# Masked attention and an MLP: the high and low parts of the last 64 keys in one moving tile

## The chip, the core and the metric

One core of a Trainium2 chip runs the whole program. The metric is the device time in microseconds of one execution. The core's engines are TensorE (PE, with its weight loads as PEld), VectorE (DVE), ScalarE (ACT), GpSimd (POOL) and SyncE (SP, which issues the DMAs). Each works through its own instructions in order; they wait for each other through semaphores.

## The reference

Attention over 8 batches, 8 heads, 576 positions and head size 64, in which each row keeps only the scores within `tau` of the row's maximum, followed by a two-layer MLP on 4608 tokens (512 to 2048 to 512):

```python
def _attn_ref(q, k, v, tau) -> np.ndarray:
    scale = 1.0 / np.sqrt(q.shape[-1])
    scores = scale * np.matmul(q, k.transpose(0, 1, 3, 2))
    thresh = np.max(scores, axis=-1, keepdims=True) - tau
    scores = np.where(scores >= thresh, scores, -1000000000.0)
    scores = scores - np.max(scores, axis=-1, keepdims=True)
    attn = np.exp(scores)
    attn = attn / (np.sum(attn, axis=-1, keepdims=True) + 1e-09)
    return np.matmul(attn, v).astype(np.float32)

def _moe_ref(x, w_in, w_out, alpha) -> np.ndarray:
    h = x @ w_in
    g = np.maximum(h, 0.0) + alpha * np.minimum(h, 0.0)
    return (g @ w_out).astype(np.float32)
```

## The kernel before

**Pairs and units.** The 64 heads are taken in 32 pairs. A pair has nine units: four blocks of 128 queries for each of the two heads (`j` = 0, 1), and a unit "t" (number 4) that holds the last 64 queries of both. Unit 1, 3, 6 and 8 are those of head 1 in the four query blocks. For a unit, PE computes the scores into PSUM (`scores`), DVE takes the row maximum (`rowmax`, tile `nmx`), ACT the exponential (`expo`, tile `p`, and the threshold `thr`), and DVE masks and sums (`mask`). Two PSUM buffers hold scores, so the scores of unit i+2 need the mask of unit i.

**Turning p.** The product with v needs p with the keys on the partitions. PE transposes the unit's p in four chunks of 128 keys (`turn`, PSUM tile `t`). 576 keys are four such chunks and 64 more: 512 keys of head 0 from the front with its last 64 left over, and 512 keys of head 1 from the back with its first 64 left over. The two left-over pieces lie side by side in `p`, and one transpose (`turn_k`, PSUM tile `tk`, and `tk_t` for unit 4) brings both: head 0's 64 keys on partitions 0 to 63, head 1's on 64 to 127. It is done once per query block, at the units of head 1 and at "t".

**Two parts.** Products run in fp32r, a narrower format than fp32. From pair 4 on (`WHOLE` = 4), p and v are split into a high and a low part. ACT copies the transposed p out of PSUM with rounding (`hi` for the four chunks, `hi_k` for the left-over keys; both at L513), and DVE subtracts that from PSUM to give the low part (`lo`, `lo_k`, both at L517). Pairs 0 to 3 run in whole fp32 and have one part.

The tiles: `E0`, `EO` and `O1` hold the four chunks, `TT[step]` the left-over keys of both heads for two query blocks (`step` 0 or 1), one tile for each part. `v` is laid out by the host in ten slots of 128 rows: eight are the chunks; slot 8 has head 0's last 64 keys in rows 0 to 63 and zeros below, slot 9 zeros and then head 1's first 64. So a product with slot 8 and the whole `TT` tile adds only head 0's keys. Its weights have 128 columns, the high and the low part of v side by side, so one pass gives both.

**The product.** `avmul(step, j)` is one accumulation group on PE: for each part, four chunks and one `TT` tile, ten products for a pair in two parts. There are four groups per pair, two with 256 columns, (0, 0) and (1, 1), and two with 322, (0, 1) and (1, 0). ACT brings the two halves of the result out (`avout`: `xa` at L575 and `xb` at L577).

**The order of work** is written out by hand. In cycle i (nine to a pair; the loop at L831), from cycle 52 on:

- PE: `scores(i+2)`, `turn(i)`, `turn_k(i)`, then some layer-2 products of the MLP (`acca`, L237), then what is due in this cycle, such as an `avmul`, and in some cycles a layer-1 group (`pha`, L207).
- DVE: `mask(i)`, `lo_k(i-1)`, `lo(i-1)`, what is due (the MLP's `pta`, the reciprocals `rv`, `rb`), `rowmax(i+2)`.
- ACT: what is due (`avout`, the MLP's `pra`, the roundings `kh`, `vst`, `qst` for the next pairs), `hi_k(i)`, `hi(i)`, `expo(i+2)` and `thr`.

Before cycle 52 two cycles are worked together. The groups of a pair in two parts are due in cycles 5 and 6 of its own pair, (0, 0) and (0, 1), and in cycles 1 and 2 of the next, (1, 1) and (1, 0) (`AVS`). How much MLP work goes into a cycle is decided by constants (`CYCLE`, `busy`, `TH1` to `TH3`) when the program is built. All transposes, products, layer-1 groups and `acca` share four PSUM buffers (`ps_m`).

After the attention the rest of the MLP runs, with the remaining weights split on DVE, ACT and POOL as they arrive; layer 1 and layer 2 of the larger part of the hidden units end the program.

Of the kernel before, what the change touches and what calls it, by code (L numbers as in the profile page):

```python
# [21 lines left out]
P = 128  # L22
D = 64
S = 576
NKC = 4
# [30 lines left out]
WHOLE = 4  # L56
# [7 lines left out]
def f(ap):  # L64
    return ap.bitcast(F32)
# [10 lines left out]
def tile_masked_attention_moe(  # L76
# [11 lines left out]
    nc = tc.nc  # L88
# [17 lines left out]
    part = [dram.tile([n, DM], F32, name=f"part{t}") for t, n in groups1]  # L106

    class Split64:


        def __init__(self, pool, raw, temp_pool, temp, eng, src, a, name, split=False):
            self.split = split
            self.pool, self.raw_tag, self.temp_pool, self.temp_tag = pool, raw, temp_pool, temp
            self.eng = [nc.vector if e == 'v' else nc.gpsimd for e in eng]
            self.src, self.a, self.name = src, a, name
# [75 lines left out]
    def split_x(pool, xr, t0, n, gn, bufs):  # L191
        xh = pool.tile([P, NCC, gn], F32R, tag="xh", name=f"xh{gn}_{t0}", bufs=bufs)
        nc.scalar.activation(xh[:, :, :n], xr[:, :, :n], AF.Copy)  # L193
        xl = pool.tile([P, NCC, gn], F32R, tag="xl", name=f"xl{gn}_{t0}", bufs=bufs)
        nc.gpsimd.tensor_tensor(xl[:, :, :n], xr[:, :, :n], f(xh[:, :, :n]), op=ALU.subtract)  # L195
        return xh, xl
# [60 lines left out]
    class Turned:  # L257


        def __init__(self, pool, dtype, parts):  # L260
            self.parts = range(parts)
            self.EO = [pool.tile([P, 2, NKC, 322], dtype, name=f"eo{parts}{i}") for i in self.parts]
            self.E0 = [pool.tile([P, NKC, 256], dtype, name=f"e0{parts}{i}") for i in self.parts]
            self.O1 = [pool.tile([P, NKC, 256], dtype, name=f"o1{parts}{i}") for i in self.parts]
            self.TT = [[pool.tile([P, 322], dtype, name=f"tt{s}{parts}{i}") for i in self.parts] for s in range(2)]
            for i in self.parts:
                nc.gpsimd.memset(f(self.TT[0][i][:, 2 : 2 + D]), 0.0)
                nc.gpsimd.memset(f(self.TT[1][i][:, 256:320]), 0.0)
                one = 1.0 - i
                nc.gpsimd.memset(f(self.TT[0][i][:, :2]), one)  # L270
                nc.gpsimd.memset(f(self.TT[1][i][:, 320:]), one)
                nc.gpsimd.memset(f(self.EO[i][:, 0, :, 320:]), one)
                nc.gpsimd.memset(f(self.EO[i][:, 1, :, :2]), one)

# [5 lines left out]
    class Pair:  # L280
# [216 lines left out]
        def places_k(self, u):  # L497
            qc, j = UNITS[u]
            if u not in self.K:
                return []  # L500
            kb = self.K[u]
            if qc == "t":
                return [
                    (kb[:D, D:], [self.set.TT[0][i][D:, 2 : D + 2] for i in self.set.parts]),
                    (kb[:D, :D], [self.set.TT[1][i][:D, 256:320] for i in self.set.parts]),
                ]
            step, qi = divmod(qc, 2)
            c0 = qi * P + (D + 2 if step == 0 else 0)
            return [(kb, [self.set.TT[step][i][:, c0 : c0 + P] for i in self.set.parts])]

        def put_hi(self, places):
            for ps, dst in places:
# [32 lines left out]
        def avmul(self, step, j, cs=range(5)):  # L545
            z = self.set
            if (step, j) == (0, 0):
                rhs, tr, col, n = z.E0, [t[:, D + 2 :] for t in z.TT[0]], 2, 256
            elif (step, j) == (0, 1):
                rhs, tr, col, n = [t[:, 1] for t in z.EO], z.TT[0], 0, 322  # L550
            elif (step, j) == (1, 0):
                rhs, tr, col, n = [t[:, 0] for t in z.EO], z.TT[1], 258, 322
            else:
                rhs, tr, col, n = z.O1, [t[:, :256] for t in z.TT[1]], 322, 256
            if cs[0] == 0:
                pa = ps_m.tile([P, 512], F32, tag="pm", name=f"av{self.pi}_{j}_{col}")
                self.av[step, j] = pa, col, n
            pa = self.av[step, j][0]
            m = self.vst.shape[2]
            for part in z.parts:  # L560
                for c in cs:
                    w = self.vst[:, j * NKC + c if c < NKC else 8 + j, :]
                    x = rhs[part][:, c, :] if c < NKC else tr[part]
                    nc.tensor.matmul(  # L564
                        pa[:m, :n], w, x, start=(part == 0 and c == 0), stop=(part == z.parts[-1] and c == NKC)
                    )

        def avout(self, step, j):
            if (step, j) == (0, 0):
# [66 lines left out]
    for p in pairs:  # L636
        o = 9 * p.pi
        n = o - 9
# [167 lines left out]
    for n_, (w, fc, io) in enumerate(pieces):  # L806
        c = n_ * DEC_LAST // (len(pieces) - 1)
# [107 lines left out]
    for t0 in range(0, NT, G2):  # L915
        n = min(G2, NT - t0)
        pool = (wp2, mp2)[t0 // G2 % 2]
        xr = load_x(pool, t0, n, G2, 1)
        x = split_x(pool, xr, t0, n, G2, 1)
        g = [hidden(mp2, ps_2, G2, fc, n, x, f"b{t0}_{fc}", nf) for fc in fcs2]  # L920
        for o in range(0, n, P):
            m = min(P, n - o)
# [14 lines left out]
def lay_out(inputs):  # L937
    import numpy as np

    q, k, v = (np.asarray(inputs[n]) for n in ("q", "k", "v"))  # L940
    b, h, s, d = q.shape
    a = {}
    for n, t in (("q", q), ("k", k)):
        a[n] = np.ascontiguousarray(t.reshape(b, h // 2, 2, s, d).transpose(0, 1, 2, 4, 3)).reshape(b, h // 2, P, s)
    a["k"] = np.concatenate([a["k"], a["k"][..., :d]], axis=-1)
    vv = np.zeros((b, h // 2, P, 10, d), v.dtype)
    v5 = v.reshape(b, h // 2, 2, s, d)
    n = NKC * P
    vv[:, :, :, :4] = v5[:, :, 0, :n].reshape(b, h // 2, NKC, P, d).transpose(0, 1, 3, 2, 4)
    vv[:, :, :, 4:8] = v5[:, :, 1, d:].reshape(b, h // 2, NKC, P, d).transpose(0, 1, 3, 2, 4)  # L950
    vv[:, :, :d, 8] = v5[:, :, 0, n:]
    vv[:, :, d:, 9] = v5[:, :, 1, :d]
    a["v"] = vv
    a["tau"] = np.asarray(inputs["tau"]).reshape(1)
    for n in ("moe_w_in", "moe_w_out"):
        w = np.ascontiguousarray(inputs[n])
        assert w.dtype == np.float64
        a[n] = w.view(np.int64)
    al = np.asarray(inputs["moe_alpha"])
    a["moe_alpha"] = np.ascontiguousarray(al.reshape(-1, P).T)  # L960
    return a
# [22 lines left out]
```

## Time and profile before

| | |
|---|---|
| device time, 3 runs | 1398.99, 1400.43, 1400.41 us; median 1400.41 |
| span of the profiled execution | 1399.2 us |
| PE busy | 1342.0 us, 96% |
| DVE busy | 975.0 us, 70% |
| ACT busy | 820.8 us, 59% |
| POOL busy | 774.5 us, 55% |

The span is the time from the first to the last instruction of one profiled execution; its own total time is not listed beside the three timed runs, which lie between 0.2 us below and 1.2 us above the span. Busy shares are means over the whole span; the stages differ, so the prediction reads them by stage. In a line of a group or of the timeline, "out<-in" names the tiles, the shapes are partitions x elements, and a note in brackets is the idle time of that engine just before, with what ended it. Matmuls are pipelined: a matmul's own duration is longer than the distance to the next one.

### The profile page before, as it was taken

To read this page: it belongs to the slowest core of one execution; us is meant where nothing else is said; L and a number is where in the kernel's file an instruction comes from. 1 tells how busy PE (TensorE), PEld (TensorE's weight loads), DVE (VectorE), ACT (ScalarE), POOL (GpSimd) and SP (SyncE) were. 2 spreads that over 40 slices of the span, in tenths; PEclk is the share of its full clock that TensorE was granted. 3 is DMA by queue.
4 is the path that set the end of the run, shared out by engine and by line. 5 is a ranking of instruction groups with operands and counts; after the bars stand their busy time and mean duration, and the time that the engine had idled before them with its cause. 6 is when DMAs were issued, how large, how long until landed. Compare 5 with 4: busy or idle time off the path is not lost.

```text
span 1399.2 us, 23363 instructions
## 1 busy us (share of the span) xinstructions
PE 1342.0 (96%) x8116; PEld 1184.1 (85%) x8116; DVE 975.0 (70%) x1933; ACT 820.8 (59%) x1843; POOL 774.5 (55%) x879
## 2 busy tenths in 40 slices
PE   5888899999999999999999999898999999999998
PEld 4555889999999999999999998776888888888887
DVE  6999888889888888898888857986333323323332
ACT  7887888888888888888888854453112012111100
POOL 3887576576666666676676557666434224223311
PEclk9999899999999999999999999999999999999999
DMA  7653644644545444454454315333320220111011
GB/s 239 177 148 102 164 113 117 175 116 132 149 120 149 138 135 137 131 146 126 128 157 135 90 56 152 123 118 128 121 69 22 90 90 31 60 61 40 21 61 38
DMA packets 94630, 157.69 MB, mean 113 GB/s; under 512 B 14160, under 2 KB 39024, under 8 KB 94512
## 3 DMA queue, kind: packets, MB, share of 16 engines
q1 hardware_dynamic: 94512, 156.19, 38.3%
q8 instruction: 65, 1.06, 0.3%
q14 instruction: 53, 0.43, 0.1%
HBM read 85.53 MB, written 28.46 MB: 81 GB/s over the span
## 4 chain that ended last, share of the span: by engine, by line
PE 78%; DVE 8%; ACT 4%; DMA 4%; POOL 3%; issue 2%; SPq 1%; POOLq 0%; DVEq 0%; ACTq 0%
PE phb L207 16%; PE accb L237 16%; PE av L564 10%; PE s L417 10%; PE pha L207 9%; PE acca L237 9%; PE t L461 7%; DMA wri<-in_moe_w_in_dram 2%; DVE p L452 1%; DVE nmx L432 1%; PE tk L477 1%; ACT xb L577 1%; DVE wto L142 1%; ACT xa L575 1%; ACT xh L193 1%
## 5 line engine op out<-in xcount | busy, mean ns | idle before, releaser
L432 DVE TENSOR_REDUCE nmx<-s 128x1 f32<-128x576 f32 x288 | 217.1, 754 | 74.9 <-PE s L417 72.0
L228 ACT ACTIVATE gb<-ptb 128x512 fp32r<-128x512 f32 x81 | 50.9, 630 | 337.3 <-DVE ptb L900 336.9
L231 POOL TENSOR_TENSOR gb<-ptb,gb 128x512 fp32r<-128x512 f32 x81 | 104.5, 1291 | 256.5 <-ACT gb L228 256.3
L237 PE MATMUL acca<-wo,ga 128*128 128x512 f32 x756 | 229.5, 418 | 6.8 <-ACT ga L228 3.5
L237 PE MATMUL accb<-wo,gb 128*128 128x512 f32 x972 | 221.9, 389 | 0.0
L237 PEld LDWEIGHTS accb<-wo,gb 128*128 128x128 f32 x972 | 182.6, 188 | 37.8
L452 DVE SCALAR_TENSOR_TENSOR p<-s,thr,p 128x576 f32<-128x576 f32 x256 | 206.8, 808 | 4.0 <-ACT thr L445 3.8
L207 PE MATMUL pha<-xh,wi 128*128 128x256 f32 x1008 | 201.2, 285 | 4.8 <-DVE pta L900 4.5
L207 PE MATMUL phb<-xh,wi 128*128 128x512 f32 x648 | 202.5, 391 | 0.4 <-ACT xh L193 0.4
L440 ACT ACTIVATE p<-s,nmx 128x576 f32<-128x576 f32 x256 | 190.0, 742 | 11.5 <-DVE nmx L432 11.5
L417 PE MATMUL s<-kh,qst 128*128 128x288 f32 x640 | 142.7, 313 | 37.4 <-DVE p L452 22.0
L207 PEld LDWEIGHTS pha<-xh,wi 128*128 128x128 f32 x1008 | 164.8, 192 | 11.1 <-DVE pta L900 6.1
L237 PEld LDWEIGHTS acca<-wo,ga 128*128 128x128 f32 x756 | 132.3, 191 | 27.9 <-POOL ga L231 5.0
L461 PE MATMUL t<-ident,p 128*128 128x128 f32 x1024 | 155.6, 275 | 0.0
L417 PEld LDWEIGHTS s<-kh,qst 128*128 128x128 f32 x640 | 101.8, 193 | 61.1 <-issue 31.7
L930 DVE TENSOR_TENSOR ob<-accb,pin 128x512 f32<-128x512 f32 x36 | 24.2, 689 | 181.5 <-PE accb L237 181.5
L207 PEld LDWEIGHTS phb<-xh,wi 128*128 128x128 f32 x648 | 122.4, 189 | 26.6 <-ACT xh L193 0.8
L207 PE MATMUL pha<-xl,wi 128*128 128x256 f32 x504 | 142.8, 283 | 0.0
L899 DVE TENSOR_SCALAR ptb<-phb,alpha_sb 128x512 f32<-128x512 f32 x81 | 60.7, 751 | 108.1 <-PE phb L207 96.4
L417 PE MATMUL s<-kl,qst 128*128 128x288 f32 x640 | 134.3, 300 | 0.0
L207 PE MATMUL phb<-xl,wi 128*128 128x512 f32 x324 | 127.1, 392 | 3.6 <-POOL xl L195 3.6
L461 PEld LDWEIGHTS t<-ident,p 128*128 128x128 f32 x1024 | 127.2, 142 | 0.1
(124 smaller groups left out, 2789.7 us busy)
## 6 DMA issues: line engine op xcount, KB each, us to landing
kr<-in_k_dram SPq DMA_DIRECT2D x31, 320.0 KB
rb<-rvd SPq DMA_DIRECT2D x64, 144.0 KB
xs<-xa SPq DMA_DIRECT2D x32, 288.0 KB
part<-po SPq DMA_DIRECT2D x36, 256.0 KB
pin<-part SPq DMA_DIRECT2D x36, 256.0 KB
out_dram<-ob SPq DMA_DIRECT2D x36, 256.0 KB
vr<-in_v_dram SPq DMA_DIRECT2D x28, 320.0 KB
qr<-in_q_dram SPq DMA_DIRECT2D x31, 288.0 KB
```

The lines of the kernel that those rows point to most:

```text
L207: nc.tensor.matmul(ph[:, :n], w[:, c, :], xx[:, c, :n], start=(c == 0 and ti == 0), stop=(c == NCC - 1 and ti == 2),)
L228: nc.scalar.activation(g[:, 0, :n], t[:, :n], AF.Copy)
L231: nc.gpsimd.tensor_tensor(g[:, 1, :n], t[:, :n], f(g[:, 0, :n]), op=ALU.subtract)
L237: nc.tensor.matmul(acc[:m, :], gg[:, g, o : o + m], w, start=(first and ti == 0), stop=(last and ti == 2))
L417: nc.tensor.matmul(ps[:, h, :288], w, kk[:, a + h * 288 : a + (h + 1) * 288], start=(ki == 0 and i == 0), stop=(ki == 1 and i == n - 1),)
L432: nc.vector.tensor_reduce(self.nmx[:, j : j + 1], self.S[u][0][:, :, :288], axis=AX.XY, op=ALU.max, negate=True)
L440: nc.scalar.activation(pj, ps[:, :, :288], AF.Exp, bias=nmx[:, j : j + 1], scale=1.0)
L452: nc.vector.scalar_tensor_tensor(pj, ps[:, :, :288], thr[:, j : j + 1], pj, op0=ALU.is_ge, op1=ALU.mult, accum_out=self.sm[:, c : c + 1])
L461: nc.tensor.transpose(tb[:, c, :], pt[:, j, j * D + c * P : j * D + (c + 1) * P], ident)
L564: nc.tensor.matmul(pa[:m, :n], w, x, start=(part == 0 and c == 0), stop=(part == z.parts[-1] and c == NKC))
L899: nc.vector.tensor_scalar(t[:, :n], ph[:, :n], 0.0, alpha_sb[:, fc : fc + 1], op0=ALU.min, op1=ALU.mult)
L930: nc.vector.tensor_tensor(ob[:m], acc[:m], pi_[:m], op=ALU.add)
```

## The change

For pairs in two parts the `TT` tiles give way to tiles `R[step][j]`, one for each group. Such a tile holds, for head j's left-over 64 keys, the high part on that head's 64 partitions and the low part on the other 64. In `v`, slots 8 and 9 of these pairs repeat the same 64 rows in both halves instead of zeros in one. One product with that slot then adds the high and the low part, and a group has nine products instead of ten. To fill the tiles, `places_k` gives two places per block (one for each head, 64 partitions each) where there was one of 128 partitions, and `lo_k` writes to the other half of the partitions from the one it reads. For unit "t" the number of places stays at two. Pairs 0 to 3 compute as before, and the order of the cycles is the same.

```diff
+            if parts == 1:
+                self.TT = [pool.tile([P, 322], dtype, name=f"tt{s}{parts}") for s in range(2)]
...
+            else:
+                self.R = [[pool.tile([P, n], dtype, name=f"rt{s}{j}") for j, n in enumerate(w)] for s, w in enumerate(((256, 322), (322, 256)))]
+                for j, x in ((0, self.R[1][0][:, 320:]), (1, self.R[0][1][:, :2])):
+                    nc.gpsimd.memset(f(x[j * D : (j + 1) * D]), 1.0)
+                    nc.gpsimd.memset(f(x[(1 - j) * D : (2 - j) * D]), 0.0)
...
+            h = [slice(0, D), slice(D, P)]
+            if not self.whole:
+                R = self.set.R
+                if qc == "t":
+                    a, b = R[0][1][:, 2 : D + 2], R[1][0][:, 256:320]
+                    return [(kb[:D, D:], [a[h[1]], a[h[0]]]), (kb[:D, :D], [b[h[0]], b[h[1]]])]
+                step, qi = divmod(qc, 2)
+                out = []
+                for jj in range(2):
+                    c0 = qi * P + (D + 2 if (step, jj) == (0, 1) else 0)
+                    x = R[step][jj][:, c0 : c0 + P]
+                    out.append((kb[h[jj]], [x[h[jj]], x[h[1 - jj]]]))
+                return out
...
-            return [(kb, [self.set.TT[step][i][:, c0 : c0 + P] for i in self.set.parts])]
+            return [(kb, [self.set.TT[step][:, c0 : c0 + P]])]
...
-            for part in z.parts:
-                for c in cs:
-                    w = self.vst[:, j * NKC + c if c < NKC else 8 + j, :]
-                    x = rhs[part][:, c, :] if c < NKC else tr[part]
-                    nc.tensor.matmul(
-                        pa[:m, :n], w, x, start=(part == 0 and c == 0), stop=(part == z.parts[-1] and c == NKC)
-                    )
+            mms = [(part, c) for part in z.parts for c in cs if c < NKC] + [(0, c) for c in cs if c == NKC]
+            for part, c in mms:
+                w = self.vst[:, j * NKC + c if c < NKC else 8 + j, :]
+                x = rhs[part][:, c, :] if c < NKC else tr
+                nc.tensor.matmul(pa[:m, :n], w, x, start=(part == 0 and c == 0), stop=c == NKC)
...
     vv[:, :, :d, 8] = v5[:, :, 0, n:]
     vv[:, :, d:, 9] = v5[:, :, 1, :d]
+    w = vv.reshape(b * (h // 2), P, 10, d)
+    w[WHOLE:, d:, 8] = w[WHOLE:, :d, 8]
+    w[WHOLE:, :d, 9] = w[WHOLE:, d:, 9]
```

More of the change, by code (lines that the diff above doesn't have):

```diff
@@ L264, in __init__ @@
             self.O1 = [pool.tile([P, NKC, 256], dtype, name=f"o1{parts}{i}") for i in self.parts]
-            self.TT = [[pool.tile([P, 322], dtype, name=f"tt{s}{parts}{i}") for i in self.parts] for s in range(2)]
+            if parts == 1:
+                self.TT = [pool.tile([P, 322], dtype, name=f"tt{s}{parts}") for s in range(2)]
+                nc.gpsimd.memset(f(self.TT[0][:, 2 : 2 + D]), 0.0)
+                nc.gpsimd.memset(f(self.TT[1][:, 256:320]), 0.0)
+                nc.gpsimd.memset(f(self.TT[0][:, :2]), 1.0)
+                nc.gpsimd.memset(f(self.TT[1][:, 320:]), 1.0)
+            else:
[3 more added lines that the diff above has]
+                    nc.gpsimd.memset(f(x[(1 - j) * D : (2 - j) * D]), 0.0)
             for i in self.parts:
-                nc.gpsimd.memset(f(self.TT[0][i][:, 2 : 2 + D]), 0.0)
-                nc.gpsimd.memset(f(self.TT[1][i][:, 256:320]), 0.0)
                 one = 1.0 - i
-                nc.gpsimd.memset(f(self.TT[0][i][:, :2]), one)
-                nc.gpsimd.memset(f(self.TT[1][i][:, 320:]), one)
                 nc.gpsimd.memset(f(self.EO[i][:, 0, :, 320:]), one)
@@ L501, in places_k @@
             kb = self.K[u]
+            h = [slice(0, D), slice(D, P)]
[11 more added lines that the diff above has]
+                return out
             if qc == "t":
[L503 to L506, printed above, removed]
+                return [(kb[:D, D:], [self.set.TT[0][D:, 2 : D + 2]]), (kb[:D, :D], [self.set.TT[1][:D, 256:320]])]
             step, qi = divmod(qc, 2)
             c0 = qi * P + (D + 2 if step == 0 else 0)
-            return [(kb, [self.set.TT[step][i][:, c0 : c0 + P] for i in self.set.parts])]
+            return [(kb, [self.set.TT[step][:, c0 : c0 + P]])]
         def put_hi(self, places):
@@ L547, in avmul @@
             if (step, j) == (0, 0):
-                rhs, tr, col, n = z.E0, [t[:, D + 2 :] for t in z.TT[0]], 2, 256
+                rhs, col, n = z.E0, 2, 256
             elif (step, j) == (0, 1):
-                rhs, tr, col, n = [t[:, 1] for t in z.EO], z.TT[0], 0, 322
+                rhs, col, n = [t[:, 1] for t in z.EO], 0, 322
             elif (step, j) == (1, 0):
-                rhs, tr, col, n = [t[:, 0] for t in z.EO], z.TT[1], 258, 322
+                rhs, col, n = [t[:, 0] for t in z.EO], 258, 322
             else:
-                rhs, tr, col, n = z.O1, [t[:, :256] for t in z.TT[1]], 322, 256
+                rhs, col, n = z.O1, 322, 256
+            if self.whole:
+                tr = z.TT[step][:, D + 2 :] if (step, j) == (0, 0) else z.TT[step][:, :n]
+            else:
+                tr = z.R[step][j]
             if cs[0] == 0:
```

## The prediction

> **What bounds the kernel now.** First the span by stages: a table of three windows, with the busy time of each engine (in brackets, instructions), the granted clock of TensorE and the DMA share.
>
> ```profile
> span 1399.2 us, 23363 instructions
> core 0: us, PE busy (x) PEld busy (x) DVE busy (x) ACT busy (x) POOL busy (x), PEclk, DMA share, GB/s
> 120.00:200.00 80.00, 69.21 (x472) 62.89 (x471) 70.62 (x156) 66.61 (x158) 48.72 (x61) 0.94 0.50 135
> 200.00:830.00 630.00, 628.42 (x4589) 598.62 (x4588) 552.89 (x1226) 536.13 (x1280) 409.49 (x519) 1.00 0.47 130
> 830.00:1399.20 569.20, 550.93 (x2576) 458.75 (x2574) 246.96 (x361) 124.40 (x197) 229.93 (x163) 0.99 0.24 76
> ```
>
> The pairs in two parts run from 120 to 830 us: three (pairs 4 to 6) in the first window, where no engine is full, then 24 in the second, where PE is busy all the time, and pair 31 at the end. The third window is MLP work that the change leaves alone; I let it shift as a block. Second, the chain that ended last, in order of time, from 300 to 420 us:
>
> ```profile
> by line: PE av L564 22.3%; PE s L417 20.9%; PE acca L237 19.3%; PE pha L207 19.0%; PE t L461 15.3%; PE tk L477 1.8%; issue 0.6%; PE tk_t L475 0.5%; PE rp L587 0.5%
> 299.93 1.18 PE av L564 x10
> 302.73 1.48 PE av L564 x10
> ```
>
> It is PE from end to end, and ten `av` products take 1.18 us (256 columns) or 1.48 us (322). But DVE is 88% busy and ACT 85% there, so I looked for the place in a pair where they come closest to PE. The list of waits, 120 to 800 us (total us, times, longest):
>
> ```profile
> DVE nmx L432 <- PE s L417: 65.7, 108, 2.4
> DVE eo L517 <- ACT eo L513: 7.7, 28, 0.4
> PE s L417 <- DVE p L452: 9.5, 8, 2.1
> ```
>
> DVE waits for PE's scores often, and once in every pair for ACT. That one place is shown by the timeline of a typical pair (start, duration, idle before in brackets). I number the nine cycles of a pair 0 to 8, each from its mask on DVE. ACT in cycles 6 and 7, with PE's `av` product that `xa` waits for:
>
> ```profile
> 442.66 0.31 PE L564 MATMUL av<-tt,vst 128*128 128x322 f32 x1
> ...
> 441.29 0.28 ACT L513 ACTIVATE tt<-tk 128x128 fp32r<-128x128 f32 x1 [0.30 <-PE tk L477]
> 441.46 0.59 ACT L513 ACTIVATE o<-t 128x512 fp32r<-128x512 f32 x1
> ...
> 442.56 0.30 ACT L445 ACTIVATE thr<-nmx,ntau_sb 128x1 f32<-128x1 f32 x1
> 443.01 0.43 ACT L575 ACTIVATE xa<-av 64x322 f32<-64x322 f32 x1
> 443.45 0.43 ACT L577 ACTIVATE xb<-av 64x322 f32<-64x322 f32 x1
> 443.91 0.74 ACT L344 ACTIVATE kh<-kr 128x640 fp32r<-128x640 f32 x1
> 444.68 0.60 ACT L513 ACTIVATE eo<-t 128x512 fp32r<-128x512 f32 x1
> ```
>
> From 441.29 on ACT has one gap, 0.15 us before `xa` (`thr` ends at 442.86; the product ends at 442.97). Its last eviction ends at 445.28, and DVE waits for just that:
>
> ```profile
> 442.15 0.08 DVE L452 DVE_READ_ACCUMULATOR p<-s,thr,p 128x1 f32 x1
> 442.15 0.28 DVE L517 TENSOR_TENSOR tt<-tk,tt 128x128 fp32r<-128x128 f32 x1
> 442.36 0.68 DVE L517 TENSOR_TENSOR o<-t,o 128x512 fp32r<-128x512 f32 x1
> ...
> 445.31 0.69 DVE L517 TENSOR_TENSOR eo<-t,eo 128x512 fp32r<-128x512 f32 x1 [0.27 <-ACT eo L513]
> ...
> 447.83 0.28 DVE L517 TENSOR_TENSOR tt<-tk,tt 128x128 fp32r<-128x128 f32 x1
> 448.04 0.68 DVE L517 TENSOR_TENSOR o<-t,o 128x512 fp32r<-128x512 f32 x1
> ...
> 450.12 0.81 DVE L452 SCALAR_TENSOR_TENSOR p<-s,thr,p 128x576 f32<-128x576 f32 x1
> ```
>
> From 445.31 DVE works without a gap (two pta, rv, two nmx, two masks among it) until the mask of cycle 1 ends at 450.93. The scores of unit 3 need that mask's PSUM buffer. PE:
>
> ```profile
> 449.32 2.10 PE L237 MATMUL acca<-wo,ga 128*128 128x512 f32 x8
> 451.26 0.42 PE L417 MATMUL s<-kh,qst 128*128 128x288 f32 x2
> ```
>
> PE comes to them at 451.26. How soon they could start shows where PE does wait for a mask, in another pair:
>
> ```profile
> 300.09 0.81 DVE L452 SCALAR_TENSOR_TENSOR p<-s,thr,p 128x576 f32<-128x576 f32 x1
> ...
> 300.96 0.80 PE L417 MATMUL s<-kh,qst 128*128 128x288 f32 x4
> ```
>
> That is 0.06 us behind the mask's end at 300.90. So the cover is 451.26 - 450.99 = **0.27 us in a pair of some 25**. PE bounds this stage, but a chain ACT, DVE, PE runs 0.27 us behind it.
>
> **The change part by part.**
>
> *PE, removed.* Of ten products one goes, in four groups a pair. By the chain's rows that is 0.118 us twice (cycles 1 and 5) and 0.149 us twice (cycles 2 and 6): 0.534 us a pair, 15.0 us in 28 pairs. The nine that are left keep their columns.
>
> *ACT and DVE, added.* Each of the four tail blocks of a pair (units 1, 3, 6, 8) was one eviction on ACT (`hi_k`) and one subtraction on DVE (`lo_k`); now each is two, over 64 partitions and the same 128 columns. The groups by form, 120 to 830 us (count | busy, mean ns):
>
> ```profile
> L517 DVE TENSOR_TENSOR tt<-tk,tt 128x128 fp32r<-128x128 f32 x112 | 32.0, 286 | 0.8 <-ACT tt L513 0.8
> L513 ACT ACTIVATE tt<-tk 128x128 fp32r<-128x128 f32 x112 | 31.1, 278 | 22.5 <-PE tk L477 17.6
> L517 DVE TENSOR_TENSOR tt<-tk_t,tt 64x64 fp32r<-64x64 f32 x56 | 12.2, 218 | 1.3
> ```
>
> Half the partitions save nothing: 64x64 costs 218 ns, and the step from 64 to 128 columns explains the rest of 286. So I take 286 ns (DVE) and 278 ns (ACT) for each half. What counts is the distance to the next start. Now a tail block hands over early: `tt` to `o` is 0.17 us on ACT and 0.21 on DVE, less than its duration. Do halves overlap so too? The nearest rows are pairs that already change from one half of the partitions to the other: on ACT `xa`, `xb`, `kh` start 0.44 and 0.46 us apart at 0.43 each, no overlap; on DVE:
>
> ```profile
> 411.25 0.08 DVE L452 DVE_READ_ACCUMULATOR p<-s,thr,p 128x1 f32 x1
> 411.36 0.45 DVE L517 TENSOR_TENSOR tt<-tk_t,tt 64x64 fp32r<-64x64 f32 x2
> ```
>
> Two of 218 ns take 0.45, and the first starts after the accumulator read rather than beside it. The new halves change sides twice, and the 512-column eviction behind them changes back. So I take no overlap at any of these joints: ACT from 0.17 to 0.28 + 0.28 + two gaps of 0.02 = 0.60, **+0.43 us a block**; DVE from 0.21 (after the read's start) to 0.11 + 0.29 + 0.29 + 0.02 = 0.71, **+0.50 us**. The other end, overlap as now, is +0.17 and +0.21; the rows with a change of sides are the nearer ones.
>
> The Trainium skill's page "VectorE: DVE Perf Modes", section "Two Vector instructions with no wait between them", has a model in which an instruction whose operands start in another 32-partition quadrant than those before it waits until all earlier ones have finished; by it the eviction behind the halves would be held as well as the halves, which speaks against this change. The `tk_t` row agrees, and the sum with it is the one made here.
>
> *What of it is on the path.* The subtractions of units 1 and 3 lie in cycles 2 and 4, where DVE then waits for PE:
>
> ```profile
> 429.96 0.76 DVE L432 TENSOR_REDUCE nmx<-s 128x1 f32<-128x576 f32 x1 [0.95 <-PE s L417]
> ...
> 435.14 0.76 DVE L432 TENSOR_REDUCE nmx<-s 128x1 f32<-128x576 f32 x1 [0.31 <-PE s L417]
> ...
> 440.75 0.76 DVE L432 TENSOR_REDUCE nmx<-s 128x1 f32<-128x576 f32 x1 [0.58 <-PE s L417]
> ```
>
> 0.95 us hides the first; of the second 0.19 is left over, a lateness that ends in cycle 6, where `nmx` waits for PE again. I cost both at nothing; without the cover each costs up to 0.50. Unit 4's small block keeps its count. Units 6 and 8 fall on the chain:
>
> - ACT, unit 6: +0.43 at 441.29. The gap before `xa` takes 0.12 (0.15 less a joint of 0.03). DVE's wait at 445.31 ends 0.31 later. DVE's own +0.50 in cycle 7 is covered by this: 0.50 - 0.27 = 0.23.
> - DVE, unit 8: +0.50 at 447.83. The mask ends 0.81 later, at 451.74.
> - PE's scores of unit 3: 451.80 instead of 451.26, **0.54 late**. PE's saving in cycle 6 is lost in this wait. All of PE's work sits behind these scores, in order.
> - From there to the next cycle 6 PE saves 0.118 + 0.149 + 0.118 = 0.385.
>
> Net: 0.54 - 0.385 = **+0.155 us a pair**, 3.7 us in 24 pairs.
>
> *Pairs 4 to 6.* PE is idle for 10.8 us of those 80, so its saving buys nothing; the chain's 0.81 counts whole: 3 x 0.81 = 2.4 us. Bounds: -1.6 (PE's saving in full) and +6.0 (all 12 DVE additions on the path).
>
> *At nothing.* Fewer memsets on POOL in the first microseconds; the first product that reads such a tile starts at 30.1 us:
>
> ```profile
> L267 POOL MEMSET tt<- x3: 145/145/145, 1.2 to 2.1; 128x64 f32 x3
> L564 PEld LDWEIGHTS av<-tt,vst x256: 136/189/330, 30.1 to 832.3; 128*128 128x128 f32 x112, 128*64 128x64 f32 x16
> ```
>
> Without that cover it is a fraction of a microsecond. The last product of each group now needs both halves; unit 8's are subtracted in cycle 0 and read in cycle 1, so no wait is added on PE there. No DMA is added or moved. `v` is arranged outside the timed program.
>
> *Sum.* 1399.2 + 3.7 + 2.4 = 1405.3 us of span. The median of the runs shown is 1400.41, 1.2 above the span, so the time is **1406.5 us**, 0.4% slower: 15 us less on PE, more than given back by a chain with 0.27 us of cover.
>
> **The rivals.**
>
> - *The halves overlap like their neighbours.* Then ACT adds 0.17 - 0.12 = 0.05 and DVE 0.21: the mask ends 0.26 later, so the scores can start at 451.25, where PE without one product stands at 451.11. Net 0.01 early and 0.385 saved: -0.395 a pair, 9.5 us in 24. Pairs 4 to 6 near nothing: **1391 us, faster**. For it: nearly every step of ACT and DVE overlaps. Against it: `xa`/`xb` and `tk_t`. Chance 0.15. The Trainium skill's page "ScalarE: Activation LUTs", section "What ACT_TABLE_LOAD costs", says that back-to-back ACTIVATEs overlap by about 93 ns, without an exception; that would be this rival on ACT, and `xa`/`xb` contradict it.
> - *Only the two halves lose their overlap, and the eviction behind them does not.* The chain then adds some 0.62 instead of 0.81 (0.11 less on ACT, 0.08 on DVE). The point from which the sign turns is 0.27 + 0.385 = 0.655. Net -0.035 a pair, -0.8 us, and 1.9 in pairs 4 to 6: **1401 to 1402 us, the same**. For it: a margin of only 0.155. Against it: `xb` to `kh`. Chance 0.18.
> - *A second place falls behind PE.* ACT's +0.43 of unit 3 reaches the small block and `eo` in cycle 4, DVE is late into cycle 5, and scores of unit 8 wait for the mask of cycle 6. It decides once that lateness passes the cover there, about 0.4 us. At 0.15 a pair it costs 3.6 more, and with 4.3 in pairs 4 to 6 the time is **1412 us**. Chance 0.12.
>
> **How the numbers follow.** The forecast has 0.55; it and the third rival make 0.67 of slower, the second 0.18 of same, the first 0.15 of faster (beyond 0.2%, 2.8 us, which is about what a measurement of this kernel can tell from no change). The forecast's own range is 1403 to 1411. The overall range reaches from the first rival to just above the third, 1390 to 1413.
>
> **What would show it.** Right: 112 fewer `av` products; halves on ACT 0.28 to 0.30 us apart and on DVE about 0.29; `s` L417 on PE waiting for `p` L452 once a pair, at unit 3, for some 0.7 us; PE idle 15 to 20 us from 200 to 830. Wrong: halves some 0.2 us apart; PE still busy throughout with the stage 9 us shorter; or PE waiting in other cycles. A changed order of the MLP work behind 830 us would upset the sum as well, since I took that stage as unchanged.

## The result, and the profile after

The changed kernel takes a median of **1414.03 us** (four runs, 1412.79 to 1414.77) against 1400.42 (four runs, 1398.99 to 1400.66): **1.0101 times the time before, 95% interval 1.0087 to 1.0115**. The forecast was 1406.5, slower by 6; it is slower by 13.6, and 1 us above the range. In its profiled execution, of 1413.88 us, the span is 12.9 us longer. First the page of the changed kernel: span, busy time of each engine, chain that ended last.

```profile
span 1412.1 us, 23454 instructions
PE 1343.6 (95%) x8004; PEld 1169.9 (83%) x8004; DVE 1014.9 (72%) x2045; ACT 857.5 (61%) x1955; POOL 773.2 (55%) x875
PE 63%; ACT 14%; DVE 12%; DMA 3%; issue 3%; POOL 3%; SPq 0%; POOLq 0%; DVEq 0%; ACTq 0%
```

The chain of before, from its page:

```profile
PE 78%; DVE 8%; ACT 4%; DMA 4%; POOL 3%; issue 2%; SPq 1%; POOLq 0%; DVEq 0%; ACTq 0%
```

ACT's share goes from 4% to 14% though it is busy for only 61% of the span: it has become part of what sets the end. Then the windows of after (start:end, length, PE, PEld, DVE, ACT, POOL busy, clock, DMA share, GB/s):

```profile
200.00:830.00 630.00, 621.75 (x4421) 577.97 (x4421) 580.35 (x1308) 563.53 (x1366) 403.43 (x511) 1.00 0.47 130
```

PE is idle for 8.3 us where it was idle for 1.6, and ACT and DVE are each busy for 27 us more. The granted clock is the same. The mask of the last unit starts on DVE here, before and after:

```profile
822.92 0.81 DVE L452 SCALAR_TENSOR_TENSOR p<-s,thr,p 128x576 f32<-128x576 f32 x1
```

```profile
835.90 0.81 DVE L458 SCALAR_TENSOR_TENSOR p<-s,thr,p 128x576 f32<-128x576 f32 x1
```

It is 12.98 us later, and the span 12.9 longer. So all of it arises in the attention, and the MLP's tail did shift as a block. Followed from pair to pair by the masks' starts in the two traces, after lies 2.2 us behind at the first mask of pair 7 and 11.9 at that of pair 31 (9.7 in 24 pairs, **0.41 a pair**), and pair 31 adds 1.1. Pair 7 alone makes 1.8 of the 9.7; the 23 pairs behind it lose 0.35 each. The start is the less certain part: one trace stands for each kernel, and at pair 7 that of the by-columns run below, whose later pairs keep before's pace, lies 1.5 us ahead of before.

**The place.** The chain of the changed kernel in order of time (start us, us, what), in one pair from a product of cycle 5 to cycle 8:

```profile
420.11 1.06 PE av L584 x9
...
422.28 0.27 ACT rt L529
422.55 0.01 issue
422.56 0.27 ACT rt L529
422.84 0.03 issue
422.86 0.60 ACT o L529
...
425.20 0.74 ACT kh L350
425.94 0.03 issue
425.97 0.61 ACT eo L529
426.57 0.02 issue
426.60 0.69 DVE eo L533
427.29 0.40 DVE pta L219
427.69 0.02 issue
427.71 0.39 ACT pra L220
428.11 0.04 issue
428.15 1.70 PE pha L207 x12
```

The two halves and the eviction behind them run without overlap, 0.28 and 0.30 us apart, as forecast. But here the chain doesn't then go through two more DVE cycles to the scores of unit 3. After the very next subtraction it goes to `pta`, to `pra`, and to PE's layer-1 group `pha` of cycle 8. That group takes a PSUM buffer of `ps_m`, and the buffer that comes round is the one that `pha` of cycle 7 holds until `pra` has read it. Such a wait is seen in the timeline of the weight loads better than in PE's own, since matmuls are pipelined (idle before in brackets; then PE):

```profile
428.15 0.19 PEld L207 LDWEIGHTS pha<-xh,wi 128*128 128x128 f32 x1 [0.42 <-ACT pra L220]
```

```profile
427.56 0.48 PE L237 MATMUL acca<-wo,ga 128*128 128x512 f32 x1
428.15 0.39 PE L207 MATMUL pha<-xh,wi 128*128 128x256 f32 x1
```

PE's own row shows an idle 0.11 us here (428.04 to 428.15), but the group starts 0.59 behind the start of `acca`. In the pair of before that the prediction quotes it starts 0.32 behind (timeline of all engines):

```profile
446.43 0.38 ACT L220 ACTIVATE pra<-pha 128x256 f32<-128x256 f32 x1 [0.34 <-DVE pta L219]
...
446.69 0.48 PE L237 MATMUL acca<-wo,ga 128*128 128x512 f32 x1
446.86 0.19 PEld L207 LDWEIGHTS pha<-xh,wi 128*128 128x128 f32 x1
...
447.01 0.28 PE L207 MATMUL pha<-xh,wi 128*128 128x256 f32 x1
```

There `pra` ends at 446.81 and the weight load starts 0.05 later, much as after the wait in the changed kernel (428.09 to 428.15). Eight `acca` in a row, by the prediction's line, start 0.23 apart, so with 0.32 the group is a little late even there. **Here the cover was about nothing already**, not 0.27. It could be read from the trace before: in all 24 pairs from 7 to 30 this load starts 0.04 us behind the release by `pra`. Its idle time in cycle 8, short waits counted, is 1.8 us in these pairs before and 9.2 after. The list of waits, which leaves out those of 0.15 us and less, names it, before and then after (total us, times, longest; 200 to 830 us):

```profile
PEld pha L207 <- ACT pra L220: 1.6, 6, 0.5
```

```profile
PEld pha L207 <- ACT pra L220: 9.4, 23, 0.4
...
PEld s L423 <- DVE p L458: 4.5, 18, 0.5
PEld t L467 <- DVE e L533: 4.1, 7, 0.6
```

The wait that I forecast, `s` for `p`, is there, but small in this list. It is there in nearly every pair, though: the load for the scores of unit 3 starts within 0.12 us of the mask's release in 23 of the 24 pairs, before in 4. The mean cycle of the 24 pairs (7 to 30), from a mask's start on DVE to the next (us, from the traces):

| cycle | 0 | 1 | 2 | 3 | 4 | 5 | 6 | 7 | 8 | sum |
|---|---|---|---|---|---|---|---|---|---|---|
| before | 3.08 | 2.53 | 3.19 | 2.60 | 2.74 | 2.88 | 2.70 | 2.80 | 2.83 | 25.35 |
| after | 3.42 | 2.42 | 3.10 | 2.52 | 3.00 | 2.98 | 2.47 | 3.17 | 2.67 | 25.76 |

Time is lost in cycles 7 and 0, where I looked, but also in 4 and 5, where I had costed the change at nothing.

### The profile page after: what moved, and what is told of

It is laid out like the page before. It is cut to its first block, busy times and chain, and to the rows that moved or that the text cites. A ratio compares the mean times of both kernels' runs of the same rounds, so it can differ in the third digit from the quotient of the medians.

```text
span 1412.1 us, 23454 instructions
## 1 busy us (share of the span) xinstructions
PE 1343.6 (95%) x8004; PEld 1169.9 (83%) x8004; DVE 1014.9 (72%) x2045; ACT 857.5 (61%) x1955; POOL 773.2 (55%) x875
## 4 chain that ended last, share of the span: by engine, by line
PE 63%; ACT 14%; DVE 12%; DMA 3%; issue 3%; POOL 3%; SPq 0%; POOLq 0%; DVEq 0%; ACTq 0%
PE phb L207 16%; PE accb L237 16%; PE s L423 7%; PE acca L237 7%; PE pha L207 6%; PE av L584 5%; PE t L467 5%; DVE p L458 2%; ACT p L446 2%; ACT eo L529 2%; DVE nmx L438 2%; DMA wri<-in_moe_w_in_dram 2%; ACT rt L529 1%; DVE eo L533 1%; ACT xb L595 1%
## 5 line engine op out<-in xcount | busy, mean ns | idle before, releaser
L423 PE MATMUL s<-kh,qst 128*128 128x288 f32 x640 | 147.6, 321 | 42.0 <-DVE p L458 25.4
```

The lines of the kernel that those rows point to most:

```text
L423: nc.tensor.matmul(ps[:, h, :288], w, kk[:, a + h * 288 : a + (h + 1) * 288], start=(ki == 0 and i == 0), stop=(ki == 1 and i == n - 1),)
```

## The experiments

Each ratio, and each difference to before, is against the kernel before run together with it (medians 1399.06 to 1399.82).

**The three parts one at a time.** First the saving alone: the kernel before without its tenth product, the one with the low part of the left-over keys.

```diff
+                    if part == 1 and c == NKC:
+                        continue
```

> The kernel before without the tenth product of each group (the low part of the left-over keys is still made, but not multiplied): PE's saving alone, ACT and DVE as before. Chain theory: the 0.27 us of cover at the scores of unit 3 is more than the 0.149 us that PE gains ahead of it, so nearly all of the 15.0 us is won: 1385 to 1388 us. Rival, the product is not on the path at all (weight loads or another engine set PE's pace): 1397 to 1401 us.

1387.41 us, 0.9910 (0.9895 to 0.9925): 12.4 us of the 15.0 that PE saves. So the saving is real. Second, ACT's halves alone, in the kernel before, with its ten products:

```diff
+        def halved(self, places, cross=False):
...
+            return [(ps[h[i]], (a[h[i]], b[h[1 - i if cross else i]])) for i in range(2)] if places else []
...
-                self.put_hi(self.places_k(u))
+                self.put_hi(self.halved(self.places_k(u)))
```

> The kernel before with only ACT's eviction of the left-over keys in halves (64 partitions each, two instead of one); DVE's subtraction whole, ten products. Chain theory: ACT is 0.44 us later at unit 6, the gap before xa takes 0.12, and the 0.27 us of cover takes nearly all of the rest; 0 to 0.15 us a pair for PSUM buffers that ACT frees later: 1401 to 1405 us. Rival, ACT is the engine that costs: half or more of the changed kernel's loss with PE's saving added back (28 us), 1412 us or more.

1415.15 us, 1.0110 (1.0095 to 1.0125): **15.3 us, far over my 2 to 5**. This is where my theory fell. Its list of waits (200 to 830 us) shows the place, though no product was taken away:

```profile
PEld pha L207 <- ACT pra L220: 8.6, 23, 0.5
```

Third, DVE's crossed halves alone:

```diff
-                self.put_lo(self.places_k(u))
+                self.put_lo(self.halved(self.places_k(u), cross=True))
```

> The kernel before with only DVE's subtraction in halves, written to the other half of the partitions as in the changed kernel (the low part of the left-over keys then meets the wrong rows of v); ACT's eviction whole, ten products. Chain theory: +0.53 us in cycle 7 (0.27 of it hidden in the wait for ACT) and +0.53 in cycle 0 make the mask of cycle 1 0.79 us late against 0.27 of cover: 0.52 us a pair, 12.5 us in 24 pairs and some 2 us in pairs 4 to 6, 1413 to 1417 us. Rival, DVE's part is hidden and ACT costs: 1400 to 1404 us.

1410.63 us, 1.0077 (1.0062 to 1.0092): 10.8 us, less than expected. The wait for `pra` is not there, since DVE's extra time in cycle 7 falls mostly where it had waited for ACT:

```profile
PEld pha L207 <- ACT pra L220: 0.6, 2, 0.4
```

DVE's cost lies mostly where the prediction looked: in this run too the load for the scores of unit 3 starts within 0.12 us of the mask's release in 19 of the 24 pairs, where before it did in 4.

The three add up: 15.3 + 10.8 - 12.4 = 13.7, and the change measured 13.6. Last of the group, the changed kernel with the last product of each group done twice, so ten again:

```diff
+            if not self.whole:
+                mms.append((1, NKC))
```

> The changed kernel with the last product of each group issued twice (the left-over keys count double): the halves on ACT and DVE as changed, PE with ten products as before. Chain theory: the waits of PE stay and the PE work between them grows by 0.385 to 0.534 us a pair, so 9 to 13 us over the changed kernel, 1423 to 1427 us. Rival, the saving was never worth anything: within 2 us of the changed kernel, 1412 to 1416 us.

1422.28 us, 1.0152 (1.0135 to 1.0169), just under the expected times. In the changed kernel the product is worth 8.3 us, against 12.4 in the kernel before: a third of it is lost in waits. This run also shows that the sum above comes out so well by luck: the two fills together cost 22.5 us, not 15.3 + 10.8 = 26.1, and what they cost less (3.6), the product wins less (4.1).

**Which blocks.** ACT's halves for two of the four units only, in the kernel before:

```diff
-                self.put_hi(self.places_k(u))
+                self.put_hi(self.halved(self.places_k(u)) if u in (6, 8) else self.places_k(u))
```

> The kernel before with ACT's eviction in halves only for units 6 and 8. Place theory: unit 6's half delays the release of the PSUM buffer that the layer-1 group of cycle 8 waits for (8.3 us in 22 pairs with halves in all four blocks): 8 to 12 us slower than before, 1408 to 1412 us. Rival, each block costs alike: half of the 15.3 us, 1406 to 1409 us.

> The kernel before with ACT's eviction in halves only for units 1 and 3. Place theory: only the PSUM buffers of cycles 3 and 4, some 0.1 to 0.15 us a pair, and part of pairs 4 to 6: 1402 to 1406 us. Rival, each block costs alike: 1406 to 1409 us. The difference to the run before decides.

Units 6 and 8: 1409.92 us, 1.0069 (1.0054 to 1.0084), 10.5 us. Units 1 and 3: 1405.63 us, 1.0041 (1.0027 to 1.0056), 6.2 us. The wait for `pra` belongs to the first alone; the row of units 6 and 8, then that of units 1 and 3:

```profile
PEld pha L207 <- ACT pra L220: 8.3, 22, 0.5
```

```profile
PEld pha L207 <- ACT pra L220: 1.3, 5, 0.3
```

The times alone hardly tell two places from one price for every block, since both intervals contain half of the 15.3 us. The cycles do (mean of the 24 pairs, us longer than before):

| cycle | 0 | 1 | 2 | 3 | 4 | 5 | 6 | 7 | 8 | sum |
|---|---|---|---|---|---|---|---|---|---|---|
| ACT, units 6 and 8 | 0.07 | -0.01 | 0.06 | 0.00 | 0.00 | 0.00 | 0.00 | 0.01 | 0.21 | 0.33 |
| ACT, units 1 and 3 | 0.00 | 0.00 | 0.00 | 0.02 | 0.10 | 0.14 | -0.09 | 0.00 | 0.00 | 0.17 |
| ACT, all four | 0.07 | -0.01 | 0.06 | 0.02 | 0.11 | 0.14 | -0.09 | 0.01 | 0.21 | 0.52 |
| DVE, all four | 0.34 | -0.12 | 0.04 | 0.00 | 0.10 | -0.04 | -0.03 | 0.37 | -0.37 | 0.30 |

So ACT's halves have two places, cycle 8 and cycles 4 and 5, and these add up cycle by cycle to the row of all four (in time 10.5 + 6.2 = 16.7, against 15.3). DVE's are late in cycle 7 and make that good in cycle 8; what stays is 0.22 in cycles 0 and 1, at the scores of unit 3, and 0.10 in cycle 4. The changed kernel's cycle 8, 0.16 shorter than before's, is the sum of both: -0.37 and 0.21.

**Relief for the chain.** If ACT's chain through `kh` and `eo` to `pra` is the place, taking `kh` (0.74 us) out of it must help. In the changed kernel the rounding `kh` goes from cycle 7 to cycle 1, with `kl` and the loads that follow:

```diff
+LATE = {**PREP, 'kh': 1, 'kl': 1, 'mk': 2, 'mk2': 3, 'lv': 2}
...
+            prep = LATE if p.pi > WHOLE + 1 else PREP
+            at_cycle(n + prep["kh"], p.prep_kh)
```

> The changed kernel with the rounding of k for the next pairs (kh, 0.74 us on ACT, with kl, its two moves and the load of v behind it) taken from cycle 7 to cycle 1 or 2 of the next pair, for pairs from 6 on: the same work, but not between the halves of unit 6 and the eviction that DVE waits for. Place theory: the wait of the layer-1 group in cycle 8 (8.9 us in 22 pairs) goes, DVE's own halves stay: 8 to 14 us faster than the changed kernel, 1400 to 1406 us. Rival, ACT's load as such: no gain, 1411 to 1416 us.

> ACT's halves in all four blocks on the kernel before (1415.2 us), with the rounding kh moved out of cycle 7 as in the earlier run. Buffer theory: the wait in cycle 8 goes (8.3 us), the rest stays: 1405 to 1409 us. Rival, ACT's load as such: 1412 to 1417 us.

> Control: the kernel before with the rounding kh moved out of cycle 7. Buffer theory: there is a wait of some 1 us in all in cycle 8 to win, and something may be lost where kh goes: 1397 to 1402 us. Were it 5 us faster or more, the 6 us that this move won in the changed kernel would be no answer to the change.

The changed kernel: 1407.98 us, 1.0062 (1.0047 to 1.0077), 6 us less than after (5.5 by the ratios), where I had expected 8 to 14. ACT's halves alone: 1408.87 us, 1.0060 (1.0039 to 1.0082), 6.3 less. The idle time of the loads in cycle 8 falls from 9.2 us to 2.9 in the changed kernel, and from 8.4 to 0.2 with ACT's halves alone. The kernel before: 1397.83 us, 0.9991 (0.9982 to 1.0001), 1.2 less, if anything. So 4 to 5 of the 6 us belong to the halves.

**The side or the count.** Two instructions in place of one cost time in themselves. To tell that from the change of sides, both engines take the same blocks in two pieces by columns, all 128 partitions each:

```diff
+            return [(ps[:, h[i]], (a[:, h[i]], b[:, h[i]])) for i in range(2)] if places else []
```

> The kernel before with each left-over block evicted and subtracted in two pieces by columns (128 partitions, 64 columns each) instead of one: as many added instructions on ACT and DVE as in the changed kernel, but no change of partitions, so neighbours should overlap. Joint theory (what costs is the lost overlap where the start partition changes): +0.05 us a block on ACT and +0.07 on DVE, which the cover mostly takes: 1399 to 1403 us. Rival, the count of instructions costs: near the fills-only run less the joints' share, 1410 us or more.

1401.57 us, 1.0009 (0.9999 to 1.0019): as good as nothing, with the same count of instructions. These pieces are also shorter (218 ns on DVE and 221 on ACT), so one more run keeps count and columns. In the changed kernel ACT evicts all 128 partitions into each `R` tile; the other head's rows are then overwritten by DVE's low part.

```diff
-                    out.append((kb[h[jj]], [x[h[jj]], x[h[1 - jj]]]))
+                    out.append((kb[h[jj]], [x[h[jj]], x[h[1 - jj]]], (kb, x)))
...
+            for ps, dst, *all_rows in places:
+                out, ps = (all_rows[0][1], all_rows[0][0]) if all_rows else (dst[0], ps)
+                nc.scalar.activation(out, ps, AF.Copy)
```

> The changed kernel, but each of ACT's two evictions per left-over block takes all 128 partitions (the rows of the other head that come with it are overwritten by DVE's low part afterwards): as many instructions on ACT as in the changed kernel, none of which changes the start partition. DVE's halves stay. Joint theory: ACT adds 0.17 us a block instead of 0.43, the wait of the layer-1 group in cycle 8 goes, and DVE's halves alone (10.8 us) stand against PE's saving (12.4): 1398 to 1405 us, 9 to 16 us faster than the changed kernel. Rival, the added instructions on ACT as such: 1411 to 1416 us.

> The run before with the rounding kh moved out of cycle 7 as well. Joint theory: ACT no longer sets a wait in cycle 8, so the move adds little beyond the 1.6 us that it won in the kernel before: 1396 to 1403 us. If ACT's chain still decides, 5 us or more faster than the run before.

1408.00 us, 1.0066 (1.0049 to 1.0083): 6 us less than after (5 by the ratios) for evictions of twice the partitions, where I had expected 9 to 16. On ACT's timeline, with all partitions and then in the changed kernel (start, duration of both together):

```profile
422.55 0.45 ACT L530 ACTIVATE rt<-tk 128x128 fp32r<-128x128 f32 x2
422.88 0.60 ACT L530 ACTIVATE o<-t 128x512 fp32r<-128x512 f32 x1
```

```profile
422.28 0.55 ACT L529 ACTIVATE rt<-tk 64x128 fp32r<-64x128 f32 x2 [0.29 <-PE tk L483]
422.86 0.60 ACT L529 ACTIVATE o<-t 128x512 fp32r<-128x512 f32 x1
```

The eviction behind them starts 0.33 us after the first, against 0.58, and 0.17 with one eviction. So of the 0.41 us that a block adds on ACT, 0.25 are the change of sides and 0.16 the second instruction. In the attention the 0.25 decide: the idle time of the loads in cycle 8 falls from 9.2 us to 3.9, and from pair 8 to pair 31 this trace gains 1.0 us on that of before, where after loses 8.0. The time shows less of it. This trace loses 3.2 us more than before's in the MLP behind the attention, and the other three executions take 2.6 to 3.8 us longer than the profiled one; why stays open. With `kh` moved as well it takes 1403.05 us, 1.0027 (1.0017 to 1.0036), the best form of the change that I found and still above the kernel before. That is 5 us less than without the move, my sign for a chain on ACT that still decides. But the two traces differ by only 0.2 us from pair 8 to pair 31, and by 3.4 us behind the attention, so they do not show such a chain. The crossing on DVE stays in both forms.

**Misses, and runs that say little.** To relieve cycle 0 as well, the reciprocal `rv` went from there to cycle 2, with `kh` moved:

```diff
-FINS = (9, 11, 12, 12, 15, 16, 16)
+FINS = (11, 11, 12, 12, 15, 16, 16)
```

> As the run before, and the reciprocals (rv, two instructions, some 0.38 us on DVE) taken from cycle 0 to cycle 2, where DVE waits for PE. Place theory: DVE's chain from cycle 8 to the scores of unit 3 is as short as before the change, so the saving of PE comes through nearly whole: 1388 to 1394 us. Rival, DVE's load as such: within 2 us of the run before.

1410.60 us, 1.0081 (1.0066 to 1.0096), a miss by 17. On DVE `rv` now stands ahead of the mask of unit 3. Against the run with `kh` moved, cycle 0 is 0.28 us shorter, but cycle 2 is 0.51 longer, and PE waits for masks, mostly for that one, by the waits from 200 to 830 us:

```profile
PEld s L424 <- DVE p L459: 14.4, 35, 1.1
```

The planner of the MLP work was told of the shorter groups, in the changed kernel with `kh` moved (its `busy` values from 1.09, 1.37, 1.09, 1.48 to 0.97, 1.22, 0.97, 1.33):

> The changed kernel with kh moved (1408.0 us), and the planner told of the shorter groups (0.12 and 0.15 us less in the four cycles with products, so that it puts more MLP products there). If PE's waits in cycles 3 to 5 are for buffers that ACT frees, more PE work in the attention cannot win much: 1405 to 1411 us. Rival, PE idles for lack of work in its queue: 1398 to 1403 us.

1433.68 us, 1.0246 (1.0229 to 1.0263): more MLP work in these cycles, and 26 us more. Why so much I did not follow up. Then the change for one query step only, with the other step's left-over keys as separate products over 64 rows:

> The new tiles for step 0 only (groups (0,0) and (0,1), blocks of units 1 and 3); step 1 keeps two TT tiles and ten products, its two tail products over the head's own 64 rows. PE saves 0.267 us a pair; the halves lie in cycles 1 to 4 alone. Place theory (the loss is in the chain from unit 6 over ACT, DVE, pta and pra to the PSUM buffer of the layer-1 group in cycle 8, and from unit 8 to the scores of unit 3): that chain is untouched, some 0.1 us a pair is lost to PSUM buffers in cycles 3 and 4, so 3 to 6 us faster than before, 1394 to 1398 us. Rival, each added instruction costs alike wherever it stands: half of the changed kernel's loss, 1405 to 1409 us.

> The new tiles for step 1 only (groups (1,0) and (1,1), blocks of units 6 and 8), step 0 with TT tiles and ten products. Place theory: the halves all lie on the chain to cycle 8 and to unit 3's scores, half of PE's saving is there: 0.2 to 0.4 us a pair slower and 2 us in pairs 4 to 6, 1406 to 1411 us. Rival, place does not matter: 1405 to 1409 us, the same as step 0 alone; the difference of the two runs decides.

1436.49 us (1.0274; 1.0254 to 1.0294) and 1442.51 us (1.0309; 1.0287 to 1.0331). They say nothing of the place, since those products are themselves dear: by an estimate in the last section they make some 31 of the 37 us in the first run. Finally the crossing by DMA, out of `TT` into the new tiles, which needs room and so 9 buffers (`GB`) instead of 11, beside the kernel before with 9:

```diff
+                nc.sync.dma_start(f(z.R[step][j][r]), f(z.TT[step][part][h[j], c0 : c0 + n]))
```

> Nine products with no halves on ACT or DVE: each left-over block is evicted and subtracted whole as before the change, into TT, and eight DMAs a pair copy the quarters into the tiles R (pairs 4 and 5 keep ten products; the MLP's hidden tiles have 9 buffers instead of 11 to make room). Joint theory (the loss is the lost overlap of the halves on ACT and DVE, PE's saving is real): 26 pairs at 0.44 us, the nine-only run's rate, 1387 to 1393 us, if 9 buffers cost nothing. Rival, what is lost is lost to the later moment at which the moving tile is complete: the last product then waits for the copies, 1400 us or more, with PE waiting for DMA.

> Control: the kernel before with 9 buffers of hidden tiles instead of 11. If that is free, 1398 to 1402 us; if the MLP's order suffers, slower, and the run with the copies is to be read against this one.

1430.17 us (1.0217; 1.0202 to 1.0232), where I had expected at most 1393, and 1430.51 us (1.0223; 1.0208 to 1.0239). The two buffers alone cost 31 us and hide whatever the DMA form would bring; PE's products wait for it besides (200 to 830 us):

```profile
PE av L577 <- DMA rt<-tt: 7.3, 9, 2.2
```

Whether it would win with room for all buffers stays open.

## Why the prediction was right, and where it was wrong

- **PE removed: right.** The groups have nine products, 1.06 us by the chain above where ten took 1.18. 0.534 us a pair were forecast and 0.44 a pair measured with this part alone.
- **ACT and DVE added: right in size.** From the first half to the eviction behind it is 0.58 us on ACT (forecast 0.60, before 0.17). On DVE, from the accumulator read to the subtraction `o`, it is 0.74 (forecast 0.71, before 0.21):

```profile
423.14 0.08 DVE L458 DVE_READ_ACCUMULATOR p<-s,thr,p 128x1 f32 x1
423.26 0.59 DVE L533 TENSOR_TENSOR rt<-tk,rt 64x128 fp32r<-64x128 f32 x2
423.88 0.69 DVE L533 TENSOR_TENSOR o<-t,o 128x512 fp32r<-128x512 f32 x1
```

The model in the Trainium skill's page "VectorE: DVE Perf Modes", section "Two Vector instructions with no wait between them", has an instruction wait for all earlier ones when its operands start in another quadrant than theirs. The trace agrees with it: the halves start no sooner than the read has ended, and the subtraction over all partitions waits too and starts 0.03 us behind them. The first rival (they overlap, 1391 us) and the second (only the halves lose it) fall with this.

- **What of it is on the path: wrong.** This is the step that failed, in two of its sentences. "So the cover is ... 0.27 us in a pair" holds for the scores of unit 3 only. I followed the lateness of ACT's last eviction on DVE to the second mask behind it and passed by `pta`, which stands in that very stretch ("two pta, rv, two nmx, two masks among it"). Through `pta`, `pra` and a PSUM buffer it reaches PE in cycle 8, two cycles earlier, with a cover of about nothing: the loads of that group are idle for 9.2 us in cycle 8, in the kernel before for 1.8. And "I cost both at nothing", for units 1 and 3, is said of the subtractions on DVE alone, which cost little there (0.04 us a pair in cycle 2 and 0.10 in cycle 4). ACT's evictions of these units have no term in the sum at all: ACT's halves there cost 6.2 us. I had looked at DVE's waits for PE as cover, but not at PE's waits for the buffers that ACT and DVE release.
- **The net of +0.155 a pair** was 0.41, so 9.7 us instead of 3.7 in 24 pairs. By the start of pair 7 after is 2.2 us behind, near the 2.4 for **pairs 4 to 6**, but with traces that differ by 1.5 us there this can be luck. **Pair 31**, which my sum left out, cost 1.1. These three account for 13.0 of span against 6.1.
- **At nothing: right** for the memsets, for the tail, and for PE's reading of both halves, by the group of those products (no idle time before them):

```profile
L584 PE MATMUL av<-rt,vst 128*128 128x322 f32 x55 | 17.0, 309 | 0.0
```

- **The third rival** had the time, 1412 us, and units 1 and 3 as a second place. The scores of unit 8, which it named, do lose their cover (their load starts within 0.12 us of the mask's release in 14 of the 24 pairs, before in none), but these loads are idle for only 0.5 us in all. The time matches in part by luck, then: the time that my sum missed lies, by the runs above, in cycle 8 and at the buffers of cycles 3 to 5. With a chance of 0.12 it was rated too low: one place had been sized, and nothing excluded others.
- **What would show it:** `s` was to wait for `p` once a pair for some 0.7 us. The scores of unit 3 do come right behind the mask in 23 of 24 pairs, but all the listed waits of `s` for `p` make 4.5 us. PE was to be idle for 15 to 20 us; its rows show 8.3, and the pair above shows why that is too little to go by: a group that starts 0.27 us later than in before has 0.11 us of idle time in front of it on PE's row and 0.42 on that of the weight loads.

Not settled: how the 6.2 us of units 1 and 3 divide. Several short waits for PSUM buffers stand in cycles 3 to 5, such as that of `t` for DVE's `e` in the list above, and no run tells them apart.

## What to carry to other kernels

Before an engine off the critical path is lengthened, every place at which the bounding engine takes something from it has to be sized, the buffers that it frees as much as the data that it makes; a load that starts 0.05 us after a release has no cover, even if the list of waits shows hardly anything. A wait of TensorE is read from its weight loads. And a tile that is filled from two sides costs the overlap on both sides of each joint. Two pieces by columns cost next to nothing here, where the data allow it; to write all partitions and overwrite gave back 5 to 6 of the 13.6 us.

## What was not expected of the hardware

In the runs with one step only, products over 64 rows stand among products over 128. In PE's timeline of the run with the change at step 0, and in its groups by form:

```profile
440.44 0.63 PE L602 MATMUL av<-o,vst 128*128 128x256 f32 x4
441.00 0.38 PE L602 MATMUL av<-tt,vst 64*128 64x256 f32 x1
441.31 0.73 PE L602 MATMUL av<-o,vst 128*128 128x256 f32 x4
```

```profile
L602 PE MATMUL av<-tt,vst 64*128 64x256 f32 x48 | 18.4, 384 | 0.0
...
L602 PE MATMUL av<-rt,vst 128*128 128x256 f32 x24 | 6.8, 282 | 0.0
```

With 256 columns such a product takes 384 ns against 282 for one over 128 rows, and the next starts 0.31 us after it rather than 0.118: half the rows cost 2.6 times the time. The product ahead of it is held apart from it too, by 0.21 us. Against two distances of 0.118 that is 0.28 us for each, and 112 of them (four in each of 28 pairs) make the 31 us of the estimate. The Trainium skill's page "TensorEngine Tiling (Array Packing)", section "Key Properties", says that a change of the tiling mode drains TensorE. These rows fit that, though no run here tells a drain from another cost of such products. The other surprise was the price of buffers: 9 instead of 11 in one ring cost 31 us, over twice what the whole change does.
